# Talking-heads attention with a gated MLP: premix on quarters of the array, mix on row halves, mix weights as one GpSimd product

## The chip, the core and the metric

The kernel runs on one core of one Trainium2 chip. The metric is the device time of one execution in microseconds (us). All engines of the core work side by side: TensorE (PE, with its weight loads as PEld), VectorE (DVE), ScalarE (ACT), GpSimd (POOL) and SyncE (SP), which issues most DMAs. TensorE multiplies a stationary operand that was loaded beforehand (up to 128 rows by 128 columns of the array) with a moving operand of up to 512 columns. A stationary operand with at most 64 rows occupies a row half of the array, one with at most 64 columns a column half, one with both a quarter.

## The reference

Eight batches, 12 heads, 448 tokens, 64 elements a head. The scores of each pair of tokens are mixed over the heads before the softmax (w_pre) and after it (w_post). Then comes an MLP with a gate over the 3584 tokens (768 to 2048 to 768).

```python
scores = scale * np.matmul(q, k.transpose(0, 1, 3, 2))
scores = np.einsum('bhij,hg->bgij', scores, w_pre)        # premix
attn = np.exp(scores - np.max(scores, axis=-1, keepdims=True))
attn = attn / (np.sum(attn, axis=-1, keepdims=True) + 1e-09)
attn = np.einsum('bhij,hg->bgij', attn, w_post)           # mix
out = np.matmul(attn, v)
...
h = x @ w_in
return (h - np.tanh(h)) @ w_out
```

All of it is float32.

## The kernel before

The attention comes first, the MLP second; the MLP's weights are rewritten as two float32r parts along the way (`narrow_steps`, lines 38 to 110, some steps per place on DVE, ACT and POOL, "the conversion").

**Blocks and groups.** A block is one batch and up to 120 of its tokens (120, 120, 120, 88). `scores` (L465) leaves a block's scores in `s`, with tokens on partitions and heads by keys along the row. Three fp32r products for each head do it, two heads side by side on the row halves of the array. The head mixing needs (token, head) pairs on partitions. So `gather` (L492) copies by DMA the rows of 10 tokens and 12 heads, 120 in all, into a tile `t` [120 x 448]. Such a group of ten tokens is the unit of the mixing; there are 360 of them, and a place `p` of the main loop (L817) handles groups 2p and 2p + 1, so there are 180 places.

**Premix.** With (token, head) on partitions, the mixing over heads is a product with a block-diagonal matrix `wpre` [120 x 120], ten copies of the 12 x 12 weights (L674 to L695 build it on POOL and DVE). `premix` (L507) makes the even group's product in float32 (L511, which the profile counts as two passes), and the odd group's as three float32r products (L514 to L516) of the upper and lower parts of `t` and of `wpre`. `split` (L498) makes the parts of `t`: the upper one on DVE (L503), the lower one on POOL (L504), a place ahead.

**Softmax and mix.** `expo` (L519) takes the row maxima from PSUM (DVE, L526) and the exponentials with their sums (ACT, L528). `norm` (L534), a place later, adds 1e-9 (L540), takes the reciprocals (L542) and scales `wpost`, the block-diagonal second weights, by them, row by row, into the mix weights `wr` (two ACT instructions, L544). `mix` (L547) multiplies the exponentials with `wr`: with `e` as the stationary operand, 112 keys at a time, so that the result has keys on partitions. That is 8 float32 products of 120 rows, 112 columns and 120 moving columns, 16 passes (L556). ACT copies the result to `at` (L565, or L572 where the groups are not whole or of one block), and `values` (L585) multiplies it with v on column halves (L597).

**Order.** A place issues in this order: gathers for place p + 2, up to six other DMAs, premix of p, norm of p - 1, split of the odd group of p + 1, expo of p, then the place's jobs, the mix of p - 1, and the conversion's steps. The copy of the mix's result is issued at the start of the next place. The jobs (transposes of q and k, `prep_q` L433 and `prep_k` L407; `scores`; `values`) are distributed over the places by due times (L735 to L804). Of the 180 places, 92 have scores (two head pairs), 22 one `values`, 29 `prep_q` and a `values`, 11 `prep_k` and a `values`, 11 a `prep_k` or `prep_q` alone, and 15 none. `in_order` (L132) then fixes the order of each engine's instructions as issued, SP's included.

**Buffers.** PSUM: two banks for the premix (`ps_p`), two for the mix (`ps_o`, one buffer), four for the jobs (`ps_m`). The even groups' `t` has three buffers, the odd groups' two.

Of the kernel before, what the change touches and what calls it, by code (L numbers as in the profile page):

```python
# [21 lines left out]
def raw(ap):  # L22

    return ap.bitcast(F32)
# [124 lines left out]
def kernel_body(  # L149
# [21 lines left out]
    GP = GI * H  # L171
    starts = list(range(0, S, MT))
# [164 lines left out]
    with ExitStack() as st:  # L337
# [152 lines left out]
        tg, ts, te = {}, {}, {}  # L490

        def gather(t, eng=nc.sync):  # L492
            i, g = groups[t]
            x = gp.tile([GP, S], F32, name="t", tag=f"t{t % 2}", bufs=3 - t % 2)
            eng.dma_start(x[: rows[t], :], sts[i][tokens[t].start : tokens[t].stop : tokens[t].step])
            tg[t] = x

        def split(t, eng=nc.gpsimd):  # L498
            n = rows[t]
            x = tg.pop(t)  # L500
            th = gp.tile([GP, S], F32R, name="th", tag="th", bufs=2)
            tl = gp.tile([GP, S], F32R, name="tl", tag="tl", bufs=2)
            nc.vector.tensor_copy(th[:n, :], x[:n, :])  # L503
            eng.tensor_sub(tl[:n, :], x[:n, :], raw(th[:n, :]))  # L504
            ts[t] = (th, tl)

        def premix(p):  # L507

            pa, pb = [ps_p.tile([P, S], F32, name="ps_p", tag="ps_p") for _ in range(2)]
            n = rows[2 * p]  # L510
            nc.tensor.matmul(pa[:n, :], wpre[:n, :n], tg.pop(2 * p)[:n, :], start=True, stop=True)  # L511
            n = rows[2 * p + 1]
            th, tl = ts.pop(2 * p + 1)
            nc.tensor.matmul(pb[:n, :], wph[:n, :n], th[:n, :], start=True, stop=False)  # L514
            nc.tensor.matmul(pb[:n, :], wpl[:n, :n], th[:n, :], start=False, stop=False)  # L515
            nc.tensor.matmul(pb[:n, :], wph[:n, :n], tl[:n, :], start=False, stop=True)  # L516
            return pa, pb

        def expo(p, pss):  # L519
            zs = gp.tile([GP, 3, 2], F32, name="zs", tag="zs")  # L520
            es = []
            for j, ps in enumerate(pss):
                n = rows[2 * p + j]

                mx = gp.tile([GP, 1], F32, name="mx", tag="mx")
                nc.vector.tensor_reduce(out=mx[:n, :], in_=ps[:n, :], axis=AX.X, op=ALU.max, negate=True)  # L526
                e = gp.tile([GP, S], F32, name="e", tag="e", bufs=4)
                nc.scalar.activation(  # L528
                    e[:n, :], ps[:n, :], AF.Exp, bias=mx[:n, :], scale=1.0, accum_out=zs[:n, 0, j : j + 1]
                )  # L530
                es.append(e)
            te[p] = [es, zs]

        def norm(p):  # L534
            zs = te[p][1]
            wr = gp.tile([GP, 2, P], F32, name="wr", tag="wr", bufs=2)[:, :, :GP]
            n0, n1 = rows[2 * p], rows[2 * p + 1]
            for j, n in enumerate((n0, n1)):

                nc.vector.tensor_scalar_add(zs[:n, 1, j : j + 1], zs[:n, 0, j : j + 1], 1e-9)  # L540
            for js, n in ((slice(0, 2), n0),) if n0 == n1 else ((slice(0, 1), n0), (slice(1, 2), n1)):
                nc.vector.reciprocal(zs[:n, 2, js], zs[:n, 1, js])  # L542
            for j, n in enumerate((n0, n1)):
                nc.scalar.mul(wr[:n, j, :], wpost[:n, :], zs[:n, 2, j : j + 1])  # L544
            te[p].append(wr)

        def mix(p):  # L547
            es, _, wr = te.pop(p)
            ps = ps_o.tile([P, 2, 512], F32, name="ps_o", tag="ps_o")
            for j, e in enumerate(es):  # L550
                i, g = groups[2 * p + j]
                n = rows[2 * p + j]
                if g == 0:
                    ats[i] = kp.tile([CP, NC, H, MT], F32, name="at", tag="at", bufs=2)
                for c in range(NC):
                    nc.tensor.matmul(  # L556
                        ps[:CP, j, c * GP : (c + 1) * GP], e[:n, c * CP : (c + 1) * CP], wr[:n, j, :],
                        start=True, stop=True,
                    )
# [90 lines left out]
        tmp_w = kp.tile([P, 2 * GP + 2 * H], F32, name="tmp_w", tag="at", bufs=2)  # L650
        w12 = tmp_w[:H, 2 * GP : 2 * GP + 2 * H].rearrange("p (w h) -> p w h", w=2)
# [11 lines left out]
        def scores_of(i, hq):  # L663
# [10 lines left out]
        repeat = tmp_w[:H, GP : 2 * GP]  # L674
        nc.gpsimd.memset(repeat, 0.0)
        nc.gpsimd.affine_select(
            out=repeat.rearrange("p (i h) -> p i h", i=GI), in_=repeat.rearrange("p (i h) -> p i h", i=GI),
            compare_op=ALU.not_equal, fill=1.0, base=0, pattern=[[0, GI], [-1, H]], channel_multiplier=1,
        )
        ps_w = bank()[:GP, : 2 * H].rearrange("p (w g) -> p w g", w=2)  # L680
        nc.tensor.matmul(ps_w.rearrange("p w g -> p (w g)"), repeat, w12.rearrange("p w g -> p (w g)"), start=True, stop=True)
        wpre, wpost = [cst.tile([GP, P], F32, name=x)[:, :GP] for x in ("wpre", "wpost")]
        pre_v = wpre.rearrange("p (i g) -> p i g", i=GI)
# [251 lines left out]
```

## Time and profile before

| | |
|---|---|
| median of 3 runs | 1862.28 us (1861.75 to 1863.77) |
| the profiled execution | 1859.88 us |
| its span, first to last instruction | 1858.2 us |
| first premix, last premix (start) | 24.5 us, 910.0 us |
| granted TensorE clock | 1.00 |
| PE busy / PEld / DVE / ACT / POOL | 99% / 82% / 66% / 59% / 25% of the span |

The page of the profile comes from one execution. Its groups of instructions are named by the line of the kernel, the engine, the operation and the tiles (out<-in), with the number of instructions, their busy time, the mean length of one in ns, and the time for which the engine had been idle before them with what ended that. A float32 product counts as two passes (two MATMUL and two LDWEIGHTS records). Matmuls are pipelined: the records of two that follow each other overlap, and the distance of their starts tells what one costs. In the timeline a row gives the start, the length, engine, line, operation and the number of instructions that were merged into it.

### The profile page before, as it was taken

The page shows a single profiled execution, that of the slowest core. Times are in us where ns is not written, and L with a number is a line of the kernel's source. Part 1 is how long each engine was busy: PE and PEld are TensorE (multiplying, and loading weights), DVE is VectorE, ACT ScalarE, POOL GpSimd, SP SyncE. Part 2 cuts the span into 40 slices and gives each one's busy share as a digit, 9 for nine tenths or more (in the row PEclk, how much of TensorE's full clock was granted, in tenths as well). Part 3 has the DMA queues.
Part 4 walks back from the last instruction along what each step waited for, and adds up shares of the span by engine and source line. Part 5 has one row for each costly group of instructions (what it writes and reads, how often), then busy time and mean ns, then how long its engine had stood idle before and what let it go on. Part 6 is the DMA issues. An engine that isn't in the chain of part 4 may idle for free.

```text
span 1858.2 us, 35351 instructions
## 1 busy us (share of the span) xinstructions
PE 1844.0 (99%) x13150; PEld 1523.0 (82%) x13150; DVE 1230.1 (66%) x2549; ACT 1099.2 (59%) x2411; POOL 455.4 (25%) x401
## 2 busy tenths in 40 slices
PE   8999999999999999999999999999999999999998
PEld 6888788788888888887788888888888888888887
DVE  5787777877787777776456556565565556556555
ACT  5877878788787887877633434434444443443433
POOL 2444445444444445444200000000000000000000
PEclk9999999999999999999999999999999999999999
DMA  8668576675765758554575665655656655655651
GB/s 179 189 185 217 167 204 197 195 220 172 225 188 169 229 180 229 178 176 151 194 297 198 224 219 196 236 202 209 231 197 218 223 207 209 218 219 194 225 202 37
DMA packets 232795, 371.92 MB, mean 200 GB/s; under 512 B 98992, under 2 KB 207536, under 8 KB 218288
## 3 DMA queue, kind: packets, MB, share of 16 engines
q1 hardware_dynamic: 231740, 368.45, 61.1%
q8 instruction: 104, 1.70, 0.4%
q10 hardware_dynamic: 884, 1.22, 0.2%
q14 instruction: 67, 0.55, 0.1%
HBM read 245.37 MB, written 47.19 MB: 157 GB/s over the span
## 4 chain that ended last, share of the span: by engine, by line
PE 95%; DMA 2%; ACT 1%; DVE 1%; issue 1%; POOL 0%; SPq 0%; ACTq 0%; POOLq 0%
PE ps_o L556 17%; PE ps_m L597 8%; PE ps_h L256 8%; PE ps_h L260 8%; PE ps_h L255 8%; PE ps_p L511 7%; PE ps_q L475 7%; PE ya L303 5%; PE ya L300 5%; PE ya L301 5%; PE yb L303 3%; PE yb L301 3%; PE yb L300 3%; PE ps_p L516 2%; PE ps_p L514 2%; PE ps_p L515 2%
## 5 line engine op out<-in xcount | busy, mean ns | idle before, releaser
L556 PEld LDWEIGHTS ps_o<-wr,e 120*112 120x112 f32 (+1 forms) x2880 | 307.2, 177 | 45.9 <-issue 29.0
L556 PE MATMUL ps_o<-wr,e 120*112 120x120 f32 (+1 forms) x2880 | 340.0, 271 | 1.6 <-ACT wr L544 1.6
L504 POOL TENSOR_TENSOR tl<-t,th 120x448 fp32r<-120x448 f32 x179 | 204.6, 1143 | 378.9 <-DVE th L503 194.0
L287 ACT CAST gh<-r 128x512 fp32r<-128x512 f32 x112 | 69.6, 621 | 374.4 <-DVE r L280 374.4
L526 DVE TENSOR_REDUCE mx<-ps_p 120x1 f32<-120x448 f32 x360 | 217.7, 621 | 105.9 <-PE ps_p L511 105.6
L256 PE MATMUL ps_h<-xl,w 128*128 128x512 f32 x672 | 263.2, 392 | 0.5 <-POOL pad L222 0.5
L255 PE MATMUL ps_h<-xh,w 128*128 128x512 f32 x672 | 262.8, 391 | 0.0
L528 ACT ACTIVATE e<-ps_p,mx 120x448 f32<-120x448 f32 x360 | 225.0, 631 | 27.9 <-DVE mx L526 26.9
L245 POOL TENSOR_TENSOR xl<-rx,xh 128x512 fp32r<-128x512 f32 x38 | 56.2, 1479 | 738.7 <-ACT xh L244 723.1
L565 ACT COPY at<-ps_o 112x960 f32<-112x960 f32 x156 | 153.6, 985 | 134.1 <-PE ps_o L556 133.0
L276 DVE SCALAR_TENSOR_TENSOR r<-qa,ps_h 128x512 f32<-128x512 f32 x112 | 77.0, 688 | 158.7 <-ACT t L273 158.7
L303 PE MATMUL ya<-w,gl 128*128 128x512 f32 x448 | 176.8, 395 | 0.7 <-DVE gl L288 0.7
L300 PE MATMUL ya<-w,gh 128*128 128x512 f32 x448 | 174.9, 390 | 1.9 <-ACT gh L287 1.9
L301 PE MATMUL ya<-w,gh 128*128 128x512 f32 x448 | 174.8, 390 | 0.0
L260 PE MATMUL ps_h<-xh,w 128*128 128x512 f32 x672 | 170.5, 389 | 0.0
L511 PE MATMUL ps_p<-t,wpre 120*120 120x448 f32 x360 | 165.3, 541 | 1.7 <-ACT e L528 0.9
L597 PE MATMUL ps_m<-at,vr 112*64 112x120 f32 (+1 forms) x3072 | 161.1, 261 | 0.0
L597 PEld LDWEIGHTS ps_m<-at,vr 112*64 112x64 f32 x3072 | 147.6, 137 | 12.9 <-issue 3.3
L270 ACT ACTIVATE u<-ps_h 128x512 f32<-128x512 f32 x112 | 66.9, 597 | 149.9 <-PE ps_h L260 149.9
L260 PEld LDWEIGHTS ps_h<-xh,w 128*128 128x128 f32 x672 | 126.1, 188 | 26.2
L256 PEld LDWEIGHTS ps_h<-xl,w 128*128 128x128 f32 x672 | 126.6, 188 | 24.6 <-POOL pad L222 0.9
L255 PEld LDWEIGHTS ps_h<-xh,w 128*128 128x128 f32 x672 | 126.6, 188 | 22.9
(102 smaller groups left out, 3623.9 us busy)
## 6 DMA issues: line engine op xcount, KB each, us to landing
w<-ws SPq DMA_DIRECT2D x112, 1536.0 KB
t<-s SPq DMA_DIRECT2D x342, 210.0 KB
cr<-in_moe_w_in_dram SPq DMA_DIRECT2D x24, 512.0 KB
cr<-in_moe_w_out_dram SPq DMA_DIRECT2D x32, 384.0 KB
vr<-in_v_dram SPq DMA_DIRECT2D x24, 448.0 KB
kr<-in_k_dram SPq DMA_DIRECT2D x23, 448.0 KB
out_dram<-ob SPq DMA_DIRECT2D x24, 384.0 KB
qr<-in_q_dram SPq DMA_DIRECT2D x23, 360.0 KB
```

The source lines that it names most:

```text
L255: nc.tensor.matmul(ph, wh[:, fs], xh, start=(c == 0), stop=False)
L256: nc.tensor.matmul(ph, wh[:, fs], xl, start=False, stop=False)
L260: nc.tensor.matmul(ph, wl[:, fs], xh, start=False, stop=(c == NK - 1))
L300: nc.tensor.matmul(y, gh[:, tok], wh[:, es], start=first, stop=False)
L301: nc.tensor.matmul(y, gh[:, tok], wl[:, es], start=False, stop=False)
L303: nc.tensor.matmul(y, gl[:, tok], wh[:, es], start=False, stop=last)
L504: eng.tensor_sub(tl[:n, :], x[:n, :], raw(th[:n, :]))
L511: nc.tensor.matmul(pa[:n, :], wpre[:n, :n], tg.pop(2 * p)[:n, :], start=True, stop=True)
L526: nc.vector.tensor_reduce(out=mx[:n, :], in_=ps[:n, :], axis=AX.X, op=ALU.max, negate=True)
L528: nc.scalar.activation(e[:n, :], ps[:n, :], AF.Exp, bias=mx[:n, :], scale=1.0, accum_out=zs[:n, 0, j : j + 1])
L556: nc.tensor.matmul(ps[:CP, j, c * GP : (c + 1) * GP], e[:n, c * CP : (c + 1) * CP], wr[:n, j, :], start=True, stop=True,)
L597: nc.tensor.matmul(pv[j * D : (j + 1) * D, r, :n], vt[:, j, c, :], ats[i][:, c, 2 * hp + j, :n], start=(c == 0), stop=(c == NC - 1),)
```

## The change

- **Gather.** Ten tokens' rows now go to partitions 4 to 123 of one of six fixed tiles in turn. Five tokens end on partitions 4 to 63, five on 64 to 123. Partitions 0 to 3 are set to zero once.
- **Premix.** Both groups are multiplied in float32, each in two pieces of five tokens: four products a place, with 64 rows and 64 columns each, on the four quarters of the array. The column half tells the group (j), the row half tells which five tokens (r), and the two row halves write to different banks. The second row half's products are issued first. The split, its tiles and the parts of `wpre` are gone.
- **Softmax.** The two banks now hold five tokens of each of the two groups, 128 partitions, and maxima and exponentials are taken over all 128.
- **Mix weights.** One GpSimd product for both banks takes the place of two ScalarE scalings; `wpost` and the reciprocals are broadcast to [128 x 2 x 60].
- **Mix.** 16 float32 products of up to 60 rows, 112 columns and 60 moving columns (32 passes) on the row halves in turn, in place of 8. The two groups are on different row halves and write to different banks; a product writes five of each ten columns.
- **Set-up.** The block-diagonal weights are built for the new partitions: eight selects, four copies and two additions in place of four selects and two copies, besides four selects for the matrix that repeats the weights, in place of one.

```diff
@@ -169,6 +169,8 @@
     GI = P // H
     MT = GI * H
     GP = GI * H
+    GH = GI // 2
+    HP = GH * H
     starts = list(range(0, S, MT))
     sizes = [min(MT, S - s) for s in starts]
     NM = len(sizes)
@@ -487,76 +489,79 @@
         tokens = {t: range(g, sizes[blocks[i][1]], ngs[blocks[i][1]]) for t, (i, g) in enumerate(groups)}
         rows = {t: H * len(x) for t, x in tokens.items()}
         at_of = {t: sum(rows[u] for u in range(t - g, t)) // H for t, (i, g) in enumerate(groups)}
-        tg, ts, te = {}, {}, {}
+        tg, te = {}, {}
+        def half_rows(t):
+            n = rows[t] // H
+            return (GH, n - GH)
+        RT = 6
+        tq = [gp.tile([P, S], F32, name="t", tag=f"t{n}", bufs=1) for n in range(RT)]
+        for x in tq:
+            nc.gpsimd.memset(x[: D - HP, :], 0.0)
         def gather(t, eng=nc.sync):
             i, g = groups[t]
-            x = gp.tile([GP, S], F32, name="t", tag=f"t{t % 2}", bufs=3 - t % 2)
-            eng.dma_start(x[: rows[t], :], sts[i][tokens[t].start : tokens[t].stop : tokens[t].step])
+            x = tq[t % RT]
+            eng.dma_start(x[D - HP : D - HP + rows[t], :], sts[i][tokens[t].start : tokens[t].stop : tokens[t].step])
             tg[t] = x
-        def split(t, eng=nc.gpsimd):
-            n = rows[t]
-            x = tg.pop(t)
-            th = gp.tile([GP, S], F32R, name="th", tag="th", bufs=2)
-            tl = gp.tile([GP, S], F32R, name="tl", tag="tl", bufs=2)
-            nc.vector.tensor_copy(th[:n, :], x[:n, :])
-            eng.tensor_sub(tl[:n, :], x[:n, :], raw(th[:n, :]))
-            ts[t] = (th, tl)
         def premix(p):
-            pa, pb = [ps_p.tile([P, S], F32, name="ps_p", tag="ps_p") for _ in range(2)]
-            n = rows[2 * p]
-            nc.tensor.matmul(pa[:n, :], wpre[:n, :n], tg.pop(2 * p)[:n, :], start=True, stop=True)
-            n = rows[2 * p + 1]
-            th, tl = ts.pop(2 * p + 1)
-            nc.tensor.matmul(pb[:n, :], wph[:n, :n], th[:n, :], start=True, stop=False)
-            nc.tensor.matmul(pb[:n, :], wpl[:n, :n], th[:n, :], start=False, stop=False)
-            nc.tensor.matmul(pb[:n, :], wph[:n, :n], tl[:n, :], start=False, stop=True)
-            return pa, pb
+            pss = [ps_p.tile([P, S], F32, name="ps_p", tag="ps_p") for _ in halves]
+            ts = [tg.pop(2 * p + j) for j in range(2)]
+            for j in (1, 0):
+                for r in (1, 0):
+                    k = slice(r * D, D + r * H * half_rows(2 * p + j)[r])
+                    nc.tensor.matmul(pss[r][halves[j], :], wpre[k, :], ts[j][k, :], start=True, stop=True)
+            return pss
         def expo(p, pss):
-            zs = gp.tile([GP, 3, 2], F32, name="zs", tag="zs")
+            zs = gp.tile([P, 3, 2], F32, name="zs", tag="zs")
             es = []
-            for j, ps in enumerate(pss):
-                n = rows[2 * p + j]
-                mx = gp.tile([GP, 1], F32, name="mx", tag="mx")
-                nc.vector.tensor_reduce(out=mx[:n, :], in_=ps[:n, :], axis=AX.X, op=ALU.max, negate=True)
-                e = gp.tile([GP, S], F32, name="e", tag="e", bufs=4)
-                nc.scalar.activation(
-                    e[:n, :], ps[:n, :], AF.Exp, bias=mx[:n, :], scale=1.0, accum_out=zs[:n, 0, j : j + 1]
-                )
+            for r, ps in enumerate(pss):
+                mx = gp.tile([P, 1], F32, name="mx", tag="mx")
+                nc.vector.tensor_reduce(out=mx, in_=ps, axis=AX.X, op=ALU.max, negate=True)
+                e = gp.tile([P, S], F32, name="e", tag="e", bufs=4)
+                nc.scalar.activation(e, ps, AF.Exp, bias=mx, scale=1.0, accum_out=zs[:, 0, r : r + 1])
                 es.append(e)
             te[p] = [es, zs]
         def norm(p):
             zs = te[p][1]
-            wr = gp.tile([GP, 2, P], F32, name="wr", tag="wr", bufs=2)[:, :, :GP]
-            n0, n1 = rows[2 * p], rows[2 * p + 1]
-            for j, n in enumerate((n0, n1)):
-                nc.vector.tensor_scalar_add(zs[:n, 1, j : j + 1], zs[:n, 0, j : j + 1], 1e-9)
-            for js, n in ((slice(0, 2), n0),) if n0 == n1 else ((slice(0, 1), n0), (slice(1, 2), n1)):
-                nc.vector.reciprocal(zs[:n, 2, js], zs[:n, 1, js])
-            for j, n in enumerate((n0, n1)):
-                nc.scalar.mul(wr[:n, j, :], wpost[:n, :], zs[:n, 2, j : j + 1])
+            wr = gp.tile([P, 2, D], F32, name="wr", tag="wr", bufs=2)[:, :, :HP]
+            for r in range(2):
+                nc.vector.tensor_scalar_add(zs[:, 1, r : r + 1], zs[:, 0, r : r + 1], 1e-9)
+            nc.vector.reciprocal(zs[:, 2], zs[:, 1])
+            nc.gpsimd.tensor_mul(
+                wr, wpost[:, :HP].unsqueeze(1).to_broadcast([P, 2, HP]), zs[:, 2].unsqueeze(2).to_broadcast([P, 2, HP])
+            )
             te[p].append(wr)
         def mix(p):
             es, _, wr = te.pop(p)
             ps = ps_o.tile([P, 2, 512], F32, name="ps_o", tag="ps_o")
-            for j, e in enumerate(es):
+            for j in range(2):
                 i, g = groups[2 * p + j]
-                n = rows[2 * p + j]
                 if g == 0:
                     ats[i] = kp.tile([CP, NC, H, MT], F32, name="at", tag="at", bufs=2)
+            for r, e in enumerate(es):
                 for c in range(NC):
-                    nc.tensor.matmul(
-                        ps[:CP, j, c * GP : (c + 1) * GP], e[:n, c * CP : (c + 1) * CP], wr[:n, j, :],
-                        start=True, stop=True,
-                    )
+                    for j, a in enumerate(halves):
+                        k = slice(a.start, a.start + H * half_rows(2 * p + j)[r])
+                        nc.tensor.matmul(
+                            ps[:CP, j, c * GP : (c + 1) * GP].rearrange("p (h i) -> p h i", i=GI)[:, :, r * GH : (r + 1) * GH],
+                            e[k, c * CP : (c + 1) * CP], wr[k, r, :],
+                            start=True, stop=True,
+                        )
             def rest():
                 (i0, _), (i1, _) = groups[2 * p], groups[2 * p + 1]
...
-        repeat = tmp_w[:H, GP : 2 * GP]
+        AT = ((D - HP, D), (0, D))
+        repeat = tmp_w[:H, : 2 * P].rearrange("p (w m) -> p w m", w=2)
...
+        for w in range(2):
+            for at in AT[w]:
+                x = repeat[:, w, at : at + HP].rearrange("p (i h) -> p i h", i=GH)
+                nc.gpsimd.affine_select(
+                    out=x, in_=x, compare_op=ALU.not_equal, fill=1.0, base=0, pattern=[[0, GH], [-1, H]],
+                    channel_multiplier=1,
+                )
+            nc.tensor.matmul(ps_w[:, w, :], repeat[:, w, :], w12[:, w, :], start=True, stop=True)
...
+        for w, x in enumerate((wpre, wpost)):
+            nc.gpsimd.memset(x[:, HP:], 0.0)
+            nc.vector.tensor_add(x[:, :HP], both[:, w, 0], both[:, w, 1])
...
-        wph, wpl = [cst.tile([GP, P], F32R, name=x)[:, :GP] for x in ("wph", "wpl")]
-        nc.vector.tensor_copy(wph, wpre)
-        nc.vector.tensor_sub(wpl, wpre, raw(wph))
...
-        split(1, nc.vector)
...
-            if p + 1 < NPL:
-                split(2 * p + 3)
```

43 lines of the change are left out of this document (22 added, 21 removed).

## The prediction

> **What bounds the kernel now.** I read the page first (span, busy times, chain), then the engines over the attention stretch, then TensorE's instructions in time, place by place.
>
> ```profile
> span 1858.2 us, 35351 instructions
> PE 1844.0 (99%) x13150; PEld 1523.0 (82%) x13150; DVE 1230.1 (66%) x2549; ACT 1099.2 (59%) x2411; POOL 455.4 (25%) x401
> ...
> PE 95%; DMA 2%; ACT 1%; DVE 1%; issue 1%; POOL 0%; SPq 0%; ACTq 0%; POOLq 0%
> ```
>
> TensorE ends the time nearly everywhere: 95% of the chain. The edit touches only the attention stretch, from the first premix to the last:
>
> ```profile
> 24.50:910.00 885.50, 884.16 (x8172) 709.87 (x8173) 671.23 (x1727) 699.21 (x1727) 396.56 (x349) 1.00 0.65 194
> ```
>
> The columns are the stretch, its length, then busy time of PE, PEld, DVE, ACT and POOL, then granted clock, DMA share and GB/s. PE is never idle in 885.5 us; ACT is busy 79%, DVE 76%, POOL 45%, DMA 65%. So here a cut in PE work is a cut in time, until ACT or DVE or a chain through them takes over. These 885.5 us are 179 steps from place to place, 4.95 us each. Three places in a row, PE only (start, length, line):
>
> ```profile
> 599.91 0.92 PE L511 MATMUL ps_p<-t,wpre 120*120 120x448 f32 x2
> ...
> 601.07 0.36 PE L516 MATMUL ps_p<-tl,wph 120*120 120x448 f32 x1
> 601.27 0.78 PE L441 MATMUL ps_m<-ident,qr 120*128 120x120 f32 x6
> 601.98 2.04 PE L597 MATMUL ps_m<-at,vr 112*64 112x88 f32 x48
> 603.95 1.90 PE L556 MATMUL ps_o<-wr,e 120*112 120x120 f32 x16
> 605.68 0.92 PE L511 MATMUL ps_p<-t,wpre 120*120 120x448 f32 x2
> ...
> 606.63 0.37 PE L515 MATMUL ps_p<-th,wpl 120*120 120x448 f32 x1
> 606.84 0.36 PE L516 MATMUL ps_p<-tl,wph 120*120 120x448 f32 x1
> 607.13 0.67 PE L475 MATMUL ps_q<-kk,qh 64*120 64x448 f32 x4
> ...
> 608.53 1.89 PE L556 MATMUL ps_o<-wr,e 120*112 120x120 f32 x16
> 610.26 0.92 PE L511 MATMUL ps_p<-t,wpre 120*120 120x448 f32 x2
> ...
> 611.63 0.93 PE L415 MATMUL ps_m<-ident,kr 112*128 112x112 f32 x8
> 612.40 1.81 PE L556 MATMUL ps_o<-wr,e 120*112 120x120 f32 x16
> 614.04 0.92 PE L511 MATMUL ps_p<-t,wpre 120*120 120x448 f32 x2
> ```
>
> Starts matter here, not lengths, since matmuls overlap. Place one is premix, prep, values, mix; place two premix, scores, mix; place three premix, prep, mix. Two kinds are still missing, a place with no job and one with values alone:
>
> ```profile
> 895.12 0.92 PE L511 MATMUL ps_p<-t,wpre 120*120 120x448 f32 x2
> ...
> 896.64 1.89 PE L556 MATMUL ps_o<-wr,e 120*112 120x120 f32 x16
> 898.37 0.92 PE L511 MATMUL ps_p<-t,wpre 120*120 120x448 f32 x2
> ...
> 899.83 2.68 PE L597 MATMUL ps_m<-at,vr 112*64 112x120 f32 x48
> 902.44 1.90 PE L556 MATMUL ps_o<-wr,e 120*112 120x120 f32 x16
> 904.17 0.92 PE L511 MATMUL ps_p<-t,wpre 120*120 120x448 f32 x2
> ```
>
> By the job plan of lines 735 to 804, the 180 places are 92 with scores, 22 with values alone, 40 with prep and values, 11 with prep alone, 15 without a job.
>
> **Step 1, prices of a change of array shape.** From L516 to L441 (both on the whole array) PE goes on after 601.27-601.07 = 0.20; from L516 to L475 (row halves) after 607.13-606.84 = 0.29. So leaving a shape costs 0.09. Entering one also lays open the first weight load:
>
> ```profile
> 607.13 0.18 PEld L475 LDWEIGHTS ps_q<-kk,qh 64*120 64x120 f32 x2 [0.31 <-ACT at L565]
> 607.23 0.18 PEld L475 LDWEIGHTS ps_q<-kk,qh 64*120 64x120 f32 x2
> 603.95 0.17 PEld L556 LDWEIGHTS ps_o<-wr,e 120*112 120x112 f32 x1
> 604.04 0.18 PEld L556 LDWEIGHTS ps_o<-wr,e 120*112 120x112 f32 x1
> ```
>
> A load of 112 columns holds the next one back by 0.09 (603.95 to 604.04). A load of 120 columns on both row halves holds the next pair back by 0.10 (607.13 to 607.23): two loads in the time of one, so row halves load side by side. For 64 columns I take 0.05, about half of 0.09.
>
> **Step 2, premix.** It goes from one f32 product and three fp32r products on the whole array to four f32 products, each on a quarter.
>
> ```profile
> L511 PE MATMUL ps_p<-t,wpre 120*120 120x448 f32 x360 | 165.3, 541 | 1.7 <-ACT e L528 0.9
> ```
>
> An f32 product is two passes of 0.54 each, 0.92 together, so the second starts 0.38 after the first and the product holds PE 0.76. The three fp32r ones take 0.20 each (606.63 to 606.84). Together 1.36, and 599.91 to 601.27 is 1.36. After: if the four quarters run at once, 0.05 of load, 0.76, and some 0.02 of issue: 0.83. No row shows a quarter. Row halves run together at full speed (loads above), and so do column halves: L597's 48 passes of 88 columns start within 1.97 (601.98 to 603.95), while the six of 120 columns of L441 take 0.71, 0.12 each; one after another the 48 would need about 3.6 to 4. The bounds are 0.83 (four at once) and 1.57 (two at once); I take 0.83, since each direction is shown by itself.
>
> **Step 3, mix.** Before, 16 passes in 608.53 to 610.26 = 1.73, less 0.09 for the first load: 1.64, 0.1025 each. After, 32 passes of 60 columns, on the two row halves in turn, into different banks: 16 pairs. Streaming halves to about 0.05, but each weight load keeps 112 columns and 0.09 to 0.095. So the load, hidden until now, becomes the price: 16 x 0.095 = 1.52. The bounds are 1.52 and an unchanged 1.64; I take 1.52. The result is written in runs of five columns; I charge nothing for that, since no pass here shows a price for how it writes.
>
> **Step 4, the sum by kind of place, PE alone.** The mix now has the shape of the scores, so scores to mix is free, but the premix has a shape of its own that each place enters and leaves (0.05, in the 0.83, and 0.09).
> - Scores: before 4.58 (605.68 to 610.26). After: 0.83 + 0.09, scores 1.40 less their exit 0.09 = 1.31, mix 1.52 + exit 0.09: 3.84. Gain 0.74, times 92: 68.1.
> - Values alone: 5.80 (898.37 to 904.17). After: 0.92 + 2.61 + (0.09 + 1.52 + 0.09): 5.23. Gain 0.57, times 22: 12.5.
> - Prep and values: 5.77. After: 0.92 + (0.71 + 0.10 first load) + 1.97 + 1.70: 5.40. Gain 0.37, times 40: 14.8.
> - Prep alone: 3.78. After: 0.92 + (0.77 + 0.10 + 0.09) + 1.70: 3.58. Gain 0.20, times 11: 2.2.
> - No job: 3.25 (895.12 to 898.37). After: 0.92 + 1.70: 2.62. Gain 0.63, times 15: 9.5.
>
> Together 107 us.
>
> **Step 5, what the other engines give back.**
>
> ```profile
> 606.63 1.23 DVE L526 TENSOR_REDUCE mx<-ps_p 120x1 f32<-120x448 f32 x2 [1.17 <-PE ps_p L511]
> ...
> 608.49 0.20 ACT L528 ACTIVATION_READ_ACCUMULATOR e<-ps_p,mx 120x1 f32 x1
> ...
> 609.72 0.17 DVE L542 RECIPROCAL zs<-zs 120x2 f32<-120x2 f32 x1
> ```
>
> The first maximum starts 0.95 after the premix starts at 605.68, and the second exponential ends at 608.69, 3.0 after. The first quarter issued now writes the second bank, so a premix waits for the second exponential of the place before, where the f32 product waited only for the first. In a scores place (3.84) that is still covered by 0.8; in a place without a job (2.62) it is not: at least 3.0.
>
> The mix weights move from ACT to POOL, and the split goes:
>
> ```profile
> L504 POOL TENSOR_TENSOR tl<-t,th 120x448 fp32r<-120x448 f32 x171 | 195.2, 1142 | 365.5 <-DVE th L503 189.3 <-issue 58.3 <-PE ps_p L516 34.7
> L544 ACT ACTIVATE wr<-wpost,zs 120x120 f32<-120x120 f32 x344 | 117.6, 393 | 1.6 <-DVE zs L542 1.0
> L503 DVE CAST th<-t 120x448 fp32r<-120x448 f32 x172 | 83.3, 484 | 28.2 <-DMA t<-s 27.8 <-issue 0.3
> L96 POOL TENSOR_TENSOR cm<-cr,cs 128x384 f32<-128x384 f32 x32 | 33.9, 1060 | 20.9 <-DVE cs L94 12.3 <-DVE zs L540 7.2 <-ACT e L528 1.4
> L96 POOL TENSOR_TENSOR cm<-cr,cs 128x512 f32<-128x512 f32 x24 | 32.0, 1334 | 33.7 <-DVE cs L94 20.7 <-DVE zs L540 9.6 <-ACT kk L426 2.3
> ```
>
> ACT loses two scalings a place (117.6 us over 344), DVE one cast of 0.48, POOL one difference of 1.14, and all that is slack. The product has 120 elements a row: by L96, 274 ns more for 128 more elements, so 1060 - 264 x 2.14 = 0.50; the far end is 1.14. I take 0.5. The Trainium skill (GPSIMD Engine Reference, Engine selection) advises against this: two-input elementwise work belongs on VectorE, GpSimd being about 2x slower, and its 2.6 cycles per element at 1.2 GHz would make 0.26 us, an estimate from that page without the fixed part. By that figure the product would be 0.24 earlier and the sum better by a few us. What decides is the queue: the product waits for the reciprocal (L542), and ahead of it in POOL's order stands the conversion's work of the place before (L96, L98 or L104, 1.0 to 1.3 each, about one a place), itself waiting for DVE or ACT; behind it stands the next conversion step, and the mix waits for the product. In a scores place the mix comes 0.92 + 1.31 = 2.2 after the premix starts, while the reciprocal is done about when it starts (609.89 against 610.26) and POOL may need 1.3 + 0.5 after that: just covered, I charge 0.1 (bounds 0 and 0.4). Without a job the mix comes 0.9 after: not covered, so I let these 15 places and the 11 with prep gain nothing. Given back: 9.2 + 9.5 + 2.2 = 21.
>
> Gathers: same count, size and queue (SP). Both of a pair now wait for one premix instead of one of them for the split in the same place, with the queue's other loads behind them; the second is needed later than now, as it was cast a place ahead. DMA share rises from 0.65 to about 0.72. Cost 0, bounds 0 and 5 us.
>
> The start has more selects and memsets on POOL, which sits idle there:
>
> ```profile
> 9.50 0.35 POOL L689 TENSOR_SCALAR_AFFINE_SELECT wpre<-wpre 120x120 f32<-120x120 f32 x1 [7.53 <-DVE wpre L685]
> ```
>
> Four selects more are 1.4 us at most, after which 24.5 - 10 us remain to the first premix; the first split's cast goes as well. Cost 0, bounds -1 and 1.5.
>
> **Sum.** 107 - 21 = 86 us off the profiled execution's 1859.88 (span 1858.2): 1774. The median of the runs, 1862.28, is 2.4 above it, so 1776.
>
> **The rivals.**
> - Mix loads in the way (ends slower). If the row halves' weight loads of f32 products go one at a time, a pair costs 0.19 instead of 0.095: 16 x 0.095 x 180 = 274 more, the 21 of waits hidden again: about 2030. It decides from a pair of 0.125 on (86 / 2880 = 0.03 above 0.095). Against it: the paired loads of L475 above. A milder form has a half's load wait for that half's own matmul: 0.145 a pair, 144 more, about 1915. The Trainium skill (TensorE: Matmul & The Clock Gate, Part 3) says just that, loads overlapping matmuls in flight only on other row groups. Against it: L556 now, on all rows, hides 0.09 of load in 0.1025. Chance of both forms 0.06.
> - Quarters only two at a time (slower): premix 1.57, 0.74 x 180 = 133 more, less hidden waits: about 1895. For it: no quarter in the trace. Chance 0.05.
> - ACT, DVE and POOL become the bound: scores places then stay at 4.2 or so, with mixes waiting for POOL behind conversion steps and mix passes of 0.1025. 0.4 x 92 = 37, and 21 more: about 1825. For it: ACT and DVE are already at 79% and 76%. Chance 0.18.
> - The gain vanishes otherwise (gathers late, DMA in some stretches full): 1850 to 1865. Chance 0.03.
>
> **How the numbers follow.** My forecast has the remaining 0.68. Without waits the sum is 1862.28 - 109, so some 1753; I go to 1750 for the start. Upwards the range takes in the third rival, to 1838; left out are the slower rivals and the vanished gain, 0.14, and some tails. About 0.2% (3.7 us) is what a measurement here can tell from no change. Faster 0.87, same 0.02, slower 0.11.
>
> **What would show it.** Right: the four premix products start within 0.05 and the next work comes some 0.9 after; mix in 16 pairs, 0.095 apart; scores places of 3.8 to 4.0; the attention stretch near 800 us; places without a job near 3.2, their mix waiting for the POOL product. Wrong: quarter passes that start 0.76 apart in twos; mix loads 0.09 apart one by one; PE idle before the mix in scores places by over 0.3; or premixes waiting for gathers.

## The result, and the profile after

| | before | after |
|---|---|---|
| median | 1862.01 us (4 runs, 1861.42 to 1863.77) | 1792.24 us (4 runs, 1788.92 to 1796.16) |
| ratio, 95% interval | | 0.9625 (0.9604 to 0.9645) |
| profiled execution, span | 1859.88, 1858.2 us | 1788.92, 1787.2 us |
| first premix, last premix (start) | 24.5, 910.0 us | 26.4, 838.2 us |

The change makes the kernel 70 us faster. The forecast was 86 us faster, 1776 with a range of 1750 to 1838. The profiled execution gains 71.0 us (1859.88 to 1788.92): the attention stretch shrinks from 885.5 to 811.8 us, 73.7 less, it starts 1.9 later, and what follows the last premix is 0.8 longer (1787.2 - 838.2 against 1858.2 - 910.0).

The page of the profile after (span; busy time, share and instructions of each engine; the chain that ended last):

```profile
span 1787.2 us, 41382 instructions
PE 1751.0 (98%) x16572; PEld 1425.6 (80%) x16572; DVE 1128.3 (63%) x2362; ACT 1000.5 (56%) x2051; POOL 320.1 (18%) x417
...
PE 87%; DMA 4%; ACT 4%; DVE 3%; issue 1%; POOL 0%; SPq 0%; ACTq 0%; DVEq 0%; POOLq 0%
```

PE's share of the chain falls from 95% to 87%: other engines and DMAs now end part of the time. The attention stretch in the same columns as before (length, busy PE, PEld, DVE, ACT, POOL, clock, DMA share, GB/s):

```profile
26.40:838.20 811.80, 788.23 (x11556) 609.75 (x11556) 569.35 (x1538) 601.13 (x1371) 256.87 (x348) 0.99 0.72 211
```

PE stands still for 23.6 us (811.8 - 788.2), where it was 1.3 before, the granted clock is 0.99 and no longer 1.00, and the DMA share is 0.72, as forecast. A scores place in time, PE only:

```profile
562.27 0.98 PE L521 MATMUL ps_p<-t,wpre 60*64 60x448 f32 x8
563.18 0.67 PE L477 MATMUL ps_q<-kk,qh 64*120 64x448 f32 x4
...
564.30 0.37 PE L477 MATMUL ps_q<-kk,ql 64*120 64x448 f32 x2
564.50 1.70 PE L560 MATMUL ps_o<-wr,e 60*112 60x60 f32 x32
566.13 0.98 PE L521 MATMUL ps_p<-t,wpre 60*64 60x448 f32 x8
```

The premix with its exit takes 0.91 (562.27 to 563.18; 0.92 forecast), the scores 1.32, the mix with its exit 1.63 (1.61 forecast), the place 3.86 (3.84 forecast). Before, the same three took 1.45, 1.40 and 1.73 (605.68, 607.13, 608.53, 610.26), so three quarters of the gain of an undisturbed place, 0.54 of 0.72, come from the premix. The eight premix passes more closely, in two narrow windows:

```profile
562.27 0.61 PE L521 MATMUL ps_p<-t,wpre 60*64 60x448 f32 x4
...
562.70 0.56 PE L521 MATMUL ps_p<-t,wpre 60*64 60x448 f32 x4
```

Four passes are under way together from 562.27 on, and the second four together from 562.70 on, 0.43 later: 0.05 of weight load and 0.38 of a pass. The quarters do run at once.

Where PE stood still in the changed kernel (who waited for what: us in total, times, longest):

```profile
PE ps_o L560 <- POOL wr L543: 7.7, 10, 1.3
PE ps_o L560 <- ACT at L570: 6.0, 9, 1.5
PE ps_m L602 <- ACT at L577: 3.1, 5, 1.0
PE ps_m L602 <- ACT at L570: 2.7, 4, 1.8
PE ps_p L521 <- DMA t<-s: 2.7, 3, 1.6
PE ps_m L602 <- DMA vr<-in_v_dram: 2.4, 2, 1.4
```

The mix (L560) waits for its weights or for the bank that the copy of the mix before has to free, `values` (L602) for that copy or for v, the premix for gathers. Of these, only the first and the gathers were in the forecast.

Place by place (from one premix start to the next, means by kind, us):

| places (number in the mean; the first and the last place left out) | before | after | gain | forecast gain, waits included |
|---|---|---|---|---|
| scores (91) | 4.59 | 3.95 | 0.65 | 0.64 |
| values alone (22) | 5.60 | 5.34 | 0.26 | 0.57 |
| prep_q and values (29) | 6.22 | 5.80 | 0.41 | 0.37 |
| prep_k and values (11) | 6.57 | 6.58 | -0.01 | 0.37 |
| prep alone (11) | 3.76 | 3.80 | -0.04 | 0 |
| no job (14) | 3.27 | 3.54 | -0.27 | 0 |

### The profile page after: what moved, and what is told of

Read it like the earlier page. It is cut to its first block, busy times and chain, and to the rows that moved or that the text cites. A ratio compares the mean times of both kernels' runs of the same rounds, so it can differ in the third digit from the quotient of the medians.

```text
span 1787.2 us, 41382 instructions
## 1 busy us (share of the span) xinstructions
PE 1751.0 (98%) x16572; PEld 1425.6 (80%) x16572; DVE 1128.3 (63%) x2362; ACT 1000.5 (56%) x2051; POOL 320.1 (18%) x417
## 4 chain that ended last, share of the span: by engine, by line
PE 87%; DMA 4%; ACT 4%; DVE 3%; issue 1%; POOL 0%; SPq 0%; ACTq 0%; DVEq 0%; POOLq 0%
PE ps_o L560 13%; PE ps_h L257 8%; PE ps_h L258 8%; PE ps_h L262 8%; PE ps_m L602 8%; PE ps_p L521 7%; PE ya L305 6%; PE ya L302 6%; PE ya L303 6%; PE ps_q L477 5%; PE yb L305 3%; PE yb L303 3%; PE yb L302 3%; DMA t<-s 2%; PE ps_m L443 1%
## 5 line engine op out<-in xcount | busy, mean ns | idle before, releaser
L560 PEld LDWEIGHTS ps_o<-wr,e 60*112 60x112 f32 (+1 forms) x5760 | 306.2, 176 | 44.3 <-POOL wr L543 21.8
L560 PE MATMUL ps_o<-wr,e 60*112 60x60 f32 (+1 forms) x5760 | 315.5, 259 | 14.3 <-POOL wr L543 7.7
L530 DVE TENSOR_REDUCE mx<-ps_p 128x1 f32<-128x448 f32 x360 | 207.7, 619 | 163.9 <-PE ps_p L521 163.7
L532 ACT ACTIVATE e<-ps_p,mx 128x448 f32<-128x448 f32 x360 | 225.7, 634 | 101.9 <-DVE mx L530 99.4
L521 PE MATMUL ps_p<-t,wpre 60*64 60x448 f32 (+1 forms) x1440 | 180.8, 569 | 3.9 <-DMA t<-s 2.7
L602 PEld LDWEIGHTS ps_m<-at,vr 112*64 112x64 f32 x3072 | 147.5, 137 | 31.0 <-ACT at L577 10.9
L602 PE MATMUL ps_m<-at,vr 112*64 112x120 f32 (+1 forms) x3072 | 161.6, 261 | 8.4 <-ACT at L577 3.1
L543 POOL TENSOR_TENSOR wr<-wpost,zs 128x120 f32<-128x120 f32 x180 | 70.2, 390 | 402.9 <-DVE zs L542 293.6
```

The costliest lines, as they stand in the source:

```text
L521: nc.tensor.matmul(pss[r][halves[j], :], wpre[k, :], ts[j][k, :], start=True, stop=True)
L530: nc.vector.tensor_reduce(out=mx, in_=ps, axis=AX.X, op=ALU.max, negate=True)
L532: nc.scalar.activation(e, ps, AF.Exp, bias=mx, scale=1.0, accum_out=zs[:, 0, r : r + 1])
L560: nc.tensor.matmul(ps[:CP, j, c * GP : (c + 1) * GP].rearrange("p (h i) -> p h i", i=GI)[:, :, r * GH : (r + 1) * GH], e[k, c * CP : (c + ...
L602: nc.tensor.matmul(pv[j * D : (j + 1) * D, r, :n], vt[:, j, c, :], ats[i][:, c, 2 * hp + j, :n], start=(c == 0), stop=(c == NC - 1),)
```

## The experiments

Each ratio is to the kernel before on the same chip; the changed kernel's is 0.9625 (0.9604 to 0.9645).

### The single parts

**e1_wr_act**: the mix weights on ScalarE again.

```diff
-            nc.gpsimd.tensor_mul(
-                wr, wpost[:, :HP].unsqueeze(1).to_broadcast([P, 2, HP]), zs[:, 2].unsqueeze(2).to_broadcast([P, 2, HP])
-            )
+            for r in range(2):
+                nc.scalar.mul(wr[:, r, :], wpost[:, :HP], zs[:, 2, r : r + 1])
```

> The changed kernel with the mix weights made by two ScalarE scalings again (128 x 60 each). Theory A (PE bound; what is lost beside PE is the mix waiting for its weights in places with few jobs, and the weights come behind ACT's copy of the mix result): each scaling about 0.3 us, so the weights are ready some 1.7 us after a premix starts, later than a mix without a job can begin (0.9), and the exponentials start up to 0.6 later; 1798 to 1812, slower than the changed kernel's 1792. Theory B (the GpSimd product behind the conversion's steps is the main loss): 1772 to 1784.

Measured: 1793.24 us, ratio 0.9642 (0.9627 to 0.9656). That overlaps the changed kernel's interval, so both theories missed: neither does it cost nor does it help. PE's waits before the mix for the weights are 14.2 us, now for ACT, in place of 13.7 for POOL and ScalarE's copy together.

**e8_before_pool**: the product alone, in the kernel before.

```diff
-            for j, n in enumerate((n0, n1)):
-                nc.scalar.mul(wr[:n, j, :], wpost[:n, :], zs[:n, 2, j : j + 1])
+            for js, n in ((slice(0, 2), n0),) if n0 == n1 else ((slice(0, 1), n0), (slice(1, 2), n1)):
+                k = js.stop - js.start
+                nc.gpsimd.tensor_mul(
+                    wr[:n, js, :], wpost[:n, :].unsqueeze(1).to_broadcast([n, k, GP]),
+                    zs[:n, 2, js].unsqueeze(2).to_broadcast([n, k, GP]),
+                )
```

> The kernel before with its mix weights as one GpSimd product and nothing else changed (240 elements a row, about 0.75 us). Theory A (ScalarE has slack while PE is the bound, so its relief alone is worth nothing): 1858 to 1866. Theory B (ScalarE's 0.67 us a place was on the path): below 1852.

Measured: 1860.08 us, ratio 0.9993 (0.9983 to 1.0002): nothing, as theory A has it. With e1 this settles the product: it is worth nothing either way round, and what is left for the gain is premix and mix. No run changes one of these two alone; their shares are read from the trace above.

**e3_before_f32**: the kernel before with both premixes in f32 on the whole array, without the split and its set-up; the odd groups' `t` gets a third buffer.

```diff
-            x = gp.tile([GP, S], F32, name="t", tag=f"t{t % 2}", bufs=3 - t % 2)
+            x = gp.tile([GP, S], F32, name="t", tag=f"t{t % 2}", bufs=3)
...
-            th, tl = ts.pop(2 * p + 1)
-            nc.tensor.matmul(pb[:n, :], wph[:n, :n], th[:n, :], start=True, stop=False)
-            nc.tensor.matmul(pb[:n, :], wpl[:n, :n], th[:n, :], start=False, stop=False)
-            nc.tensor.matmul(pb[:n, :], wph[:n, :n], tl[:n, :], start=False, stop=True)
+            nc.tensor.matmul(pb[:n, :], wpre[:n, :n], tg.pop(2 * p + 1)[:n, :], start=True, stop=True)
...
-            if p + 1 < NPL:
-                split(2 * p + 3)
```

> The kernel before with both groups' premix as one f32 product on the whole array, and no split. Theory A (the gain is the four quarters at once, not the missing split): the premix goes from 1.36 to 1.52 us, 0.16 x 180 = 29 more; 1885 to 1895. Theory B (dropping the split's work on VectorE and GpSimd is what helped): below 1862.

Measured: 1882.08 us, ratio 1.0118 (1.0103 to 1.0133): 22 slower, 3 short of theory A's band and far from B. Its premix, PE in time:

```profile
609.09 0.92 PE L511 MATMUL ps_p<-t,wpre 120*120 120x448 f32 x2
609.85 0.92 PE L513 MATMUL ps_p<-t,wpre 120*120 120x448 f32 x2
610.69 0.67 PE L475 MATMUL ps_q<-kk,qh 64*120 64x448 f32 x4
```

Two f32 products hold PE 1.60 with the exit (609.09 to 610.69), against 1.45 before and 0.91 on quarters. So freeing VectorE and GpSimd of the split gains nothing while PE is the bound; the quarters do.

**e2_mix120**: twice the streaming in the mix. The products of the second row half overwrite those of the first, and a product now writes whole runs of columns.

```diff
-    ps[:CP, j, c * GP : (c + 1) * GP].rearrange("p (h i) -> p h i", i=GI)[:, :, r * GH : (r + 1) * GH],
-    e[k, c * CP : (c + 1) * CP], wr[k, r, :],
+    ps[:CP, j, c * GP : (c + 1) * GP],
+    e[k, c * CP : (c + 1) * CP], wr[k, :, :],
```

> The changed kernel with 120 moving columns in every mix product instead of 60 (both halves' weights; the second row half's products overwrite the first's, so the mix sums only five of the ten tokens' rows correctly and the output is not the reference's). Theory A (a mix pair is bound by its 112-column weight load of 0.095): streaming grows from 0.05 to 0.10 a pass, so a pair goes from 0.095 to 0.1025; 16 x 0.0075 x 180 = 22 more, 1808 to 1820. Theory B (a pair is bound by streaming or by the number of instructions and something per column): 0.05 more a pair, up to 144 more, 1880 to 1936.

Measured: 1795.90 us, ratio 0.9656 (0.9642 to 0.9671): below both theories' bands; its interval overlaps the changed kernel's. The mix in time:

```profile
567.24 1.80 PE L560 MATMUL ps_o<-wr,e 60*112 60x120 f32 x32
568.97 0.98 PE L521 MATMUL ps_p<-t,wpre 60*64 60x448 f32 x8
```

1.73 in place of 1.63, so twice the columns cost 0.10, where 0.12 was worked out for a pair bound by its weight load and 0.8 for one bound by streaming. So streaming is not the price. A fixed price of some 0.05 for each instruction would look the same in this run; against it, the 48 passes of `values` start within 1.97 in the kernel before (601.98 to 603.95), 0.041 each. That leaves the weight load. The runs of five columns, which this edit takes away too, are not told apart by it, but 1.63 against a forecast of 1.61 without a price for them leaves little room for one.

0.10 x 180 = 18 us of PE work cost 3.7 by the medians, whose intervals overlap, and 9.2 by the profiled executions (1798.13, the slowest of e2's four runs, against 1788.92, the fastest of the changed kernel's four). In the latter PE's standstill in the attention stretch fell from 23.6 to 20.2 us and its time at half clock from 17.1 to 10.2 us (the last section shows such stretches). So part of the added PE work was covered by waits; how large a part, these runs do not settle.

### What was given back

**e4_norm_early** and **e7_wr_dve** try theory A, that the product stands badly in GpSimd's queue. In e4, reciprocals and product are issued before the conversion's steps of their own place; in e7 the product is VectorE's.

```diff
 # e4
-            if 1 <= p < NPL + 1:
-                norm(p - 1)
...
+            if p < NPL:
+                norm(p)
             if 4 <= p < NPL:
                 conv.place()
 # e7
-            nc.gpsimd.tensor_mul(
+            nc.vector.tensor_mul(
```

> The changed kernel with the sums' reciprocals and the GpSimd product issued at the end of their own place, ahead of the conversion's steps, instead of in the next place behind them. Theory A (the mixes wait for the product because it stands behind conversion steps on GpSimd and their feeders on VectorE): most of the 16 us of waits before the mix go, and with them some of the stretches at half clock; 1774 to 1784. Theory B (those places are bound by the chain premix, maximum, exponential, premix of 3.0 us): within 4 us of 1792.

> The changed kernel with the mix weights as one VectorE product, right behind the reciprocals on VectorE. Theory A (the product's place in the queue counts, not the engine's speed): the product is no longer behind conversion steps on GpSimd but 0.3 us is added to VectorE a place; waits before the mix shrink; 1778 to 1788. Theory B (GpSimd is no cause): 1790 to 1798.

Measured: e4 1819.75 us, ratio 0.9774 (0.9747 to 0.9802), 27 slower than the changed kernel; e7 1803.44 us, ratio 0.9682 (0.9661 to 0.9702), 11 slower. Theory A fails in both, and theory B's bands (within 4 of 1792; 1790 to 1798) are missed too: neither had the edit down as a loss. PE's waits in e4, its attention stretch, and then waits of VectorE and ScalarE there:

```profile
PE ps_o L560 <- ACT at L570: 19.1, 23, 2.1
PE ps_m L602 <- ACT at L577: 8.7, 7, 2.7
PE ps_m L602 <- ACT at L570: 4.0, 3, 3.7
...
26.00:871.20 845.20, 807.94 (x11556) 624.30 (x11556) 575.78 (x1538) 601.79 (x1371) 270.55 (x349) 0.97 0.69 202
...
DVE zs L541 <- ACT e L532: 103.2, 185, 2.6
...
ACT cs L102 <- POOL cm L98: 38.3, 27, 3.0
...
ACT cm L82 <- DVE cm L80: 7.0, 8, 2.3
```

The wait for the product is gone (1.2 us of it is left), but the mix's wait for ScalarE's copy of the mix before grew from 6.0 to 19.1 us, and the clock fell to 0.97. The trace shows the links. VectorE now waits for the sums of the exponentials at the end of its place (103.2 us; 6.1 in the changed kernel). The product, and the conversion's L98 behind it on GpSimd, come late with it; ScalarE's L102 waits for L98 (38.3 us; 0.6 in the changed kernel), and the copy stands behind L102 in ScalarE's queue. The way through VectorE's L80 and ScalarE's L82 is there too, but smaller (7.0 us; 2.1).

**e5_late_values** and **e6_both** give the copy one place more before `values`; e6 is e5 with e4.

```diff
-                halved.append(((f1 - 1) // 2 + 2, f2 // 2 + 1 if f2 < NG else NPL + 7, "v", i, x))
+                halved.append(((f1 - 1) // 2 + (3 if f1 < NG else 2), f2 // 2 + 1 if f2 < NG else NPL + 7, "v", i, x))
```

> The changed kernel with every values job due one place later (but for the last block's). Theory A (the first values of a block waits for ScalarE's copy of the last mix result, which the shorter premix no longer covers): the 7 us of waits before values go, and some half-clock time; 1780 to 1788. Theory B (these waits only move, or places get worse elsewhere, since the mix result's buffers are freed later): 1789 to 1796.

> Early reciprocals and product, and values a place later, together. Theory A (waits add): 1764 to 1776, and the TensorE clock granted at 1.00 nearly throughout, since PE no longer stands still for over a microsecond. Theory B (one bound behind the other): 1780 or more.

Measured: e5 1792.20 us, ratio 0.9628 (0.9614 to 0.9643), the same; e6 1802.70 us, ratio 0.9683 (0.9666 to 0.9699), 10 slower than the changed kernel but 17 faster than e4 alone. Theory B's bands hold in both. In e5 no wait of `values` for the copy is left among PE's longest, yet PE stands still as long in total (22.8 us in the stretch, 23.6 in the changed kernel): mixes wait more for their weights (9.1 us, 7.7 in the changed kernel), premixes for the copies (2.7, 1.0) and scores for the parts of k (2.8, 0.5). The waits moved.

**A third theory, late DMAs.** The longest place of the changed kernel that begins a chain of stalls runs from 51.56 to 59.61, 8.05 where 6.15 is usual:

```profile
51.56 0.98 PE L521 MATMUL ps_p<-t,wpre 60*64 60x448 f32 x8
51.86 0.43 DVE L80 TENSOR_SCALAR cm<-cr 128x512 f32<-128x512 f32 x1 [0.90 <-DMA cr<-in_moe_w_in_dram]
...
53.27 0.43 DVE L80 TENSOR_SCALAR cm<-cr 128x512 f32<-128x512 f32 x1 [0.98 <-DMA cr<-in_moe_w_in_dram]
...
53.74 0.63 ACT L82 ACTIVATE cm<-cm 128x512 f32<-128x512 f32 x1 [0.78 <-DVE cm L80]
54.27 0.96 ACT L570 COPY at<-ps_o 112x960 f32<-112x960 f32 x1
...
55.28 2.68 PE L602 MATMUL ps_m<-at,vr 112*64 112x120 f32 x48 [1.82 <-ACT at L570]
```

Read it downwards: a chunk of the conversion has not landed; VectorE stands; ScalarE's next step stands; the copy behind that is late; `values` and PE wait 1.82. The conversion takes a load for landed one place after it was sent (L58), and places are now shorter. VectorE's waits for DMAs in the attention stretch of the changed kernel:

```profile
DVE cs L87 <- DMA ws<-cs: 6.9, 3, 3.5
DVE cm L80 <- DMA cr<-in_moe_w_in_dram: 3.4, 4, 1.0
DVE x L620 <- DMA xs<-x: 2.4, 1, 2.4
DVE cm L80 <- DMA cr<-in_moe_w_out_dram: 1.6, 2, 1.2
```

**e9_landed2** aims at the waits at L80, **e10_bufs3** at those at L87, **e11_landed2_bufs3** at both. **e12_half_gathers** makes all DMA lighter: it leaves out the gathers of the odd groups after the third, so that half of the tokens' results are wrong, with the same work on the engines.

```diff
 # e9, e11
-            if not landed(1):
+            if not landed(2):
 # e10, e11
-    s = pool.tile([p, CW], I32, name="cs", tag="cs", bufs=2)[:, :n]
+    s = pool.tile([p, CW], I32, name="cs", tag="cs", bufs=3)[:, :n]
...
-    fl = pool.tile([p, CW], F32R, name="cl", tag="cl", bufs=2)[:, :n]
+    fl = pool.tile([p, CW], F32R, name="cl", tag="cl", bufs=3)[:, :n]
 # e12, in gather
-            eng.dma_start(x[D - HP : D - HP + rows[t], :], sts[i][tokens[t].start : tokens[t].stop : tokens[t].step])
+            if t % 2 == 0 or t < RT:
+                eng.dma_start(x[D - HP : D - HP + rows[t], :], sts[i][tokens[t].start : tokens[t].stop : tokens[t].step])
```

> The changed kernel with a conversion chunk begun two places after its load was issued instead of one. Theory C (the gain lost beside PE comes from DMAs that land too late for the shorter places: VectorE then stands at the conversion's first step and all behind it, the maxima and reciprocals, too): the 3.4 us of VectorE's waits for chunk loads go and what follows from them; 1782 to 1789. Theory D (the engines' chains alone, DMA no cause): 1790 to 1796.

> The changed kernel with three buffers instead of two for the conversion's two result tiles, so that VectorE's step at L87 no longer waits for the store of two chunks before. Theory C: the 6.9 us of waits at L87 go and what follows from them; 1780 to 1788. Theory D: 1790 to 1796.

> Both of these together. Theory C: 1772 to 1782. Theory D: 1790 to 1796.

> The changed kernel without the gathers of the odd groups after the third (their premix reads the old contents of the tile, so half the tokens' results are wrong); work on all engines and in every place is the same, only DMA traffic and SP's queue are lighter by some 0.12 of DMA share. Theory C (late DMAs): the waits for DMA on VectorE (14 us) and PE (5 us) and the stalls that follow shrink to a few us; 1764 to 1776, with the clock at 1.00. Theory D: 1788 to 1796.

Measured: e9 1795.30 us, ratio 0.9643 (0.9623 to 0.9662); e10 1791.97 us, 0.9633 (0.9619 to 0.9647); e11 1799.82 us, 0.9677 (0.9656 to 0.9698); e12 1783.44 us, 0.9584 (0.9568 to 0.9599). e9 tests little, since 4.3 us of waits at L80 are left of 5.0. In e10 VectorE's waits for DMAs fell from 14.3 to 5.9 us, and the time did not move. In e11 they fell to 6.2 us, and it is 10 us slower than the changed kernel, outside both theories. So the conversion's own waits are not what costs, against theory C. e12, its attention stretch and what VectorE still waits for:

```profile
26.10:831.60 805.50, 787.86 (x11556) 610.44 (x11557) 567.88 (x1538) 600.85 (x1371) 257.18 (x348) 0.99 0.58 166
...
DVE cm L80 <- DMA cr<-in_moe_w_in_dram: 0.6, 1, 0.6
```

With the DMA share at 0.58 in place of 0.72 and the work on all engines the same, VectorE's waits for DMAs are nearly gone, and so are PE's for v. That is worth 8 us (0.9625 - 0.9584 of 1861), half of the least that theory C had; 1783 lies between the two theories' bands. It comes in places with values: by means, prep_k and values goes from 6.58 to 6.31, values alone from 5.34 to 5.20. The scores places do not change (3.95 and 3.94). The clock stays at 0.99, where theory C wanted 1.00.

No variant that computes the whole result beats the changed kernel.

**All runs by one account.** Take the attention stretch of each profiled execution, and take off the time in which PE stood still (length less busy PE) and half of the time at half clock, since PE then does about half as much (the place at 109.23 in the last section takes 1.56 us longer, with 3.4 us at half clock). What is left is PE's own work at full clock, an estimate from these figures (us):

| run | stretch | PE stood still | at half clock | what is left |
|---|---|---|---|---|
| before | 885.5 | 1.3 | 0 | 884.2 |
| changed | 811.8 | 23.6 | 17.1 | 779.7 |
| e2 | 823.9 | 20.2 | 10.2 | 798.6 |
| e4 | 845.2 | 37.3 | 51.2 | 782.3 |
| e5 | 816.6 | 22.8 | 34.0 | 776.8 |
| e6 | 830.9 | 27.6 | 47.8 | 779.4 |
| e11 | 826.3 | 28.2 | 37.5 | 779.3 |
| e12 | 805.5 | 17.6 | 17.1 | 779.3 |

The last column is the same, within 6 us, for all runs with the same products, and 19 us more for e2, where 18 were worked out. So standstill and clock are all that sets these variants apart; e11 loses 10 us to the clock alone, and e12 gains its time by 6.0 us less of standstill.

## Why the prediction was right, and where it was off

- **What bounds the kernel: right, and it ran out.** Cutting PE cut the time, and e3 and e8 show that relief of the other engines alone does not. After the cut PE is no longer alone: in e2, 18 us of PE work cost 3.7 by the medians and 9.2 by the profiled executions.
- **Step 1, changes of shape: right.** The exit from the quarters is 0.48 from the second passes to the scores (562.70 to 563.18), 0.38 of pass and 0.10; the mix behind the scores has none.
- **Step 2, quarters at once: right**, 0.91 for 0.92. The rival of two at a time is refuted by the four passes at 562.27.
- **Step 3, a mix pair costs its weight load: right**, 1.63 for 1.61, and e2 rules out streaming as the price. The rival of loads one by one, 0.19 a pair, is refuted. So is its milder form, the Trainium skill's rule that loads overlap matmuls in flight only on other row groups (TensorE: Matmul & The Clock Gate, Part 3): it would have made 16 pairs of 0.145, 2.32 a mix.
- **Step 4, the sum by places: right for the scores places**, 3.86 for 3.84, which carry 59 of the stretch's 73.7 us. PE's own work fell by 104.5 us (884.2 - 779.7) for 107. (The range's lower end starts from 109 where the sum is 107; nothing hangs on it.)
- **Step 5, what is given back: the term that was mis-sized.** It was put at 21 us; by the profiled executions it is 36 (107 - 71). 2.5 of these are PE work that did not go, 2.7 lie ahead of the first and behind the last premix, and 30.8 are in the stretch: 22.3 more of PE standing still, and some 8.5 for the halved clock, which the step did not have at all. Scores places were charged 0.1 for waiting on POOL, and 0.09 is what they lost (3.95 against 3.86 undisturbed). That fits by luck: the mix behind scores hardly waits, and 14.4 of the 17.1 us at half clock fell on scores places, behind stalls in the places before them. Places without a job, put at no gain, lost 0.27 each, 4 us. Places with values alone and with prep_k and values, to which step 5 charged nothing, fell 0.31 and 0.38 short, 11 us; PE stood still in them for 8.4 us, mostly at L602 for ScalarE's copies (5.8) and for v (2.4). I had not seen that the premix covers ScalarE's copy of the last mix for a block's first `values`, and that a premix of 0.91 in place of 1.45 no longer does. Part of it is late DMA: with half of the gathers, 6 of the 11 us come back.
- **The GpSimd product: priced at 0.5, it takes 0.39.** To make it elsewhere or earlier gains nothing: on ScalarE (e1) the time is the same, and on VectorE (e7) or issued earlier (e4) it is worse.
- **Gathers and DMA: put at 0 to 5 us.** e12 shows 8 for the half of the gathers. Premixes did wait for gathers, which was named as a sign of being wrong, but only three times, 2.7 us in all.
- **The start: put at -1 to 1.5 us**, the first premix comes 1.9 later.
- **The third rival** (ACT, DVE and POOL become the bound, 1825) has part of the truth in a milder form: ACT and DVE end 7% of the chain now, where it was 2%, and DMAs 4%, where it was 2%.

Open: what would take the standstill away. e4, e5 and e6 show waits moving from one in-order queue to the next. One possible cause is left that no run tests: the conversion's steps on ScalarE, ahead of the copy of the mix. At 107.52, where PE waits 1.50 for that copy:

```profile
104.26 0.85 PE L560 MATMUL ps_o<-wr,e 60*112 60x60 f32 x14
...
105.03 0.66 ACT L82 ACTIVATE cm<-cm 128x512 f32<-128x512 f32 x1
...
105.86 0.65 ACT L85 ACTIVATE cr<-cr 128x512 f32<-128x512 int32 x1 [0.17 <-DVE cr L83]
...
106.42 0.96 ACT L570 COPY at<-ps_o 112x960 f32<-112x960 f32 x1
```

The mix ends at 105.11, but the copy starts 1.31 later, behind L82 and L85. Of the 14 waits of PE for ScalarE's copies of over 0.3 us, 11 have one to three conversion steps just ahead of the copy on ScalarE. What it is worth to issue them behind the copy is not shown.

## What to carry to other kernels

A product with at most 64 rows and 64 columns can share the array with three others: four f32 products took the time of one. When streaming is cut in half, look for the weight load behind it, which then sets the pace. Price a cut on the bounding engine also by what its length covered: copies, loads and chains that were hidden under it come out one after another, and to remove one of them can move the wait to the next. Add what a stall does to the clock.

## What the hardware showed that was not expected

The clock. In the kernel before it was granted at 1.00 through the attention; in the changed one it was halved in four stretches between the first and the last premix, 17.1 us in all (three of 3.4 us and one of 6.8), which by the halved rate lost some 8.5 us, an estimate. One case, PE in time and then the window (columns as above, the clock is the third number from the end):

```profile
105.04 0.98 PE L521 MATMUL ps_p<-t,wpre 60*64 60x448 f32 x8
107.52 1.78 PE L560 MATMUL ps_o<-wr,e 60*112 60x60 f32 x32 [1.50 <-ACT at L570]
109.23 1.58 PE L521 MATMUL ps_p<-t,wpre 60*64 60x448 f32 x8
...
109.40:112.90 3.50, 3.50 (x20) 1.93 (x18) 1.77 (x3) 2.24 (x6) 1.41 (x2) 0.51 0.60 220
```

PE stood still for 1.50 us before a mix without a job ahead of it; from 109.5 on, for 3.4 us, the clock was halved; and the next place took 5.42 in place of 3.86. At 721.84 a gap of 1.01 was followed by the same. The Trainium skill (TensorE: Matmul & The Clock Gate, Why this matters for your kernels) warns of idle gaps over about 3 us; here gaps of 1.0 and 1.5 came before it. So a stall of PE can cost again as much as it lasted.

It need not. The stretch's longest gap, 1.82 before 55.28, was followed by no halved clock. By the trace's clock records the halved stretches of the attention and the one just behind it start at 27.57, 109.49, 723.89, 795.57 and 843.35; the distances are 24, 180, 21 and 14 times 3.413 us, as if the clock were set in slots of that length. In the slot ahead of each start PE stood still for 1.63, 1.45, 1.01, 1.26 and 1.16 us. The gap before 55.28 lies across a border of such slots, with 1.41 in the first; that slot, and others with 1.40 and 1.24, were followed by none. So how much standstill in a slot it takes is not settled here; with less than 1.0 in a slot the clock was never halved in this trace.
